# Cosine attention and feed-forward on one core: 64x128 TensorE products cut into 64x64 ones, and an uneven cut of the last output half

## The chip, the core and the metric

The kernel runs on one core of a Trainium2 chip. Its time is the device time of one execution in microseconds; the kernel before takes 405.37 us (median of 3 runs, 405.29 to 405.46). A profile of one execution gives each engine's instructions with their starts: PE is TensorE (PEld its weight loads), DVE is VectorE, ACT is ScalarE, POOL is GpSimd, SP is SyncE, which here only issues transfers.

## What is computed

Eight batches of twelve heads, 448 positions, 64 dimensions a head. Queries and keys are normalised, multiplied, divided by tau = 0.1 and put through a softmax; the result times the values is a matrix of 3584 tokens by 768, which goes through two dense layers with a leaky ReLU between them.

```python
def _attn_ref(q, k, v, tau):
    q_n = q / (np.linalg.norm(q, axis=-1, keepdims=True) + 1e-06)
    k_n = k / (np.linalg.norm(k, axis=-1, keepdims=True) + 1e-06)
    scores = np.matmul(q_n, k_n.transpose(0, 1, 3, 2)) / tau
    scores = scores - np.max(scores, axis=-1, keepdims=True)
    attn = np.exp(scores)
    attn = attn / (np.sum(attn, axis=-1, keepdims=True) + 1e-09)
    return np.matmul(attn, v).astype(np.float32)      # q, k, v: (8, 12, 448, 64)

def _moe_ref(x, w_in, w_out):                         # x: (3584, 768)
    h = x @ w_in                                      # (768, 2048)
    g = np.maximum(0.01 * h, h)
    return (g @ w_out).astype(np.float32)             # (2048, 768)
```

## The kernel before

The order of all work is written out by hand; no planner moves anything. Matrix operands are bfloat16, sums are float32 in PSUM, which is dealt out bank by bank (512 columns of 128 rows, eight banks) by `banks` (L75), the oldest free ones first.

**Heads come in pairs.** A slot s is a pair of heads of one batch; its normalised queries and keys lie transposed in `qkT[s]`, head 0 in rows 0 to 63, head 1 in rows 64 to 127, with 448 query columns (384 and 64) followed by the keys. A *key tile* (`key_tiles`, L268) multiplies a block of keys by all queries of the pair and hands the two banks that it fills to one exponential on ACT (L292). For ki = 0, 1, 2 the block is 128 keys: two matmuls, one per head, with 64 contraction rows and 128 output columns of the array ("64x128"), which run side by side, since they use different rows of the array. For ki = 3 the remaining 64 keys of two neighbouring slots share a tile: four matmuls of 64 rows and 64 columns ("64x64").

**Attention of a batch** (`attend_all`, L675) forms the sums over the exponentials and the products with the values, in matmuls of 64 rows by 32 columns, eight at a time (L719), and then 128 by 32, four at a time (L321). ACT turns the sums into reciprocals, DVE scales into `xT` (L366).

**The dense layers** run by chunks c = 0 to 7 of 384 (even c) or 512 tokens (odd c). The first layer (`first`, L379) accumulates six 128x128 matmuls for each of 16 blocks m of d_ff (L389); ACT applies the leaky ReLU into `hT[c]` (L396). The second layer of chunks 0 to 6 is done in *visits* (`visit`, L776), between the first layer and the next batch's attention. A visit begins with two or three key tiles of kind 3, then interleaves `groups` (L447) with the next batch's 18 key tiles of kinds 0 to 2, at steps listed in `wide`, `three`, `four` and `four_late` (L796 to L799); in the first two visits another key tile of kind 3 stands at the end.

A group takes 128 tokens and both halves of 384 output columns. Each block m of 128 contraction rows is cut in two row halves h, which run side by side into two banks (L464): in the first 16 steps, rows 0 to 63 add to bank 0 and rows 64 to 127 to bank 1; then they change banks, behind a wait on the last matmul of each (L463, `behind`, L205: an empty PE instruction that waits). Two key tiles stand before that wait in every group of this kind. In the first visit two pairs of banks are worked at once, in four parts. At the end DVE or ACT copies the banks out (L476) and SP stores them.

**The last chunk** (c = 7) has no next batch: `second` (L415) runs 128x128 matmuls over 16 blocks (L426), a half of 384 columns at a time, each followed by a DVE copy (L432) and, from the second half on, a store (L441). The very last half is cut into two parts of 192 columns, each copied and stored by itself; of the two transfers of a part, the first is issued on SP and the second on ACT.

**Queues near the change.** PE runs its instructions in the order written, each matmul behind a load of its weights. SP issues the loads of q and k, the transposes by DMA, and the stores. POOL issues the loads of values and weights; the last part of w_out lands while the first visit runs.

Of the kernel before, what the change touches and what calls it, by code (L numbers as in the profile page):

```python
# [16 lines left out]
def kernel(  # L17
# [11 lines left out]
    B, H, S, D = q.shape  # L29
# [12 lines left out]
    HALF = D_model // 2  # L42
# [32 lines left out]
    def banks(count, keep=None, which=None):  # L75
        lo, hi = (0, 8) if not deals["apart"] else (0, 4) if count == 2 else (4, 8)
        x = which if which is not None else min(
            (i for i in range(lo, hi, count) if not set(range(i, i + count)) & set(sum(kept.values(), []))),
            key=lambda i: max(age[i : i + count]),
        )  # L80
        deals["n"] += 1
        age[x : x + count] = [deals["n"]] * count
        if keep:
            kept[keep] = list(range(x, x + count))
        return ps[:, x] if count == 1 else ps[:, x : x + count]

    def given_back(keep):
        deals["n"] += 1
        for i in kept.pop(keep):
            age[i] = deals["n"]  # L90
# [114 lines left out]
    def behind(eng, ins, why):  # L205

        tc.add_manual_dep(
            eng.nop().ins, ins.ins.name,
            mybir.DependencyInfo(mybir.DependencyClass.Sync, mybir.DependencyReason.DATA),
            reason=why,  # L210
        )
# [53 lines left out]
    def scores(s, kis):  # L265
        key_tiles([(s, ki) for ki in kis])

    def key_tiles(which):  # L268

        tiles = []  # L270
        for s, ki in which:
            sc = banks(2)
            tiles.append(sc)
            for i in range(2 if ki == 3 else 1):
                x = qkT[s - 1 + (i ^ s // 2 % NQ % 2)] if ki == 3 else qkT[s]
                for a in range(2):
                    rows = slice(64 * a, 64 * a + 64)
                    out = sc[64 * i : 64 * i + 64] if ki == 3 else sc
                    c0, c1 = (448, 512) if ki == 3 else (512 + 128 * ki, 640 + 128 * ki)
                    nc.tensor.matmul(  # L280
                        out=out[:, a, :S], lhsT=x[rows, c0:c1], rhs=x[rows, 0:S],
                        start=True, stop=True,
                    )
        for (s, ki), sc in zip(which, tiles):
            if ki == 3:
                pr[s // 2] = prp.tile([128, 2, S], BF16, name="pr")
                dst = pr[s // 2]
            else:
                if s not in pe:
                    pe[s] = pep.tile([128, 3, 2, S], BF16, name="pe")  # L290
                dst = pe[s][:, ki]
            nc.scalar.activation(out=dst, in_=sc[:, :, :S], func=AF.Exp, scale=inv_tau)  # L292
# [80 lines left out]
    hT = {}  # L373

    def chunk_cols(c):
        return (0, MAIN) if c % 2 == 0 else (MAIN, 512)
# [27 lines left out]
    def rows_of(c, x, end):  # L404

        bb, rest = divmod(x, S)
        r0 = (2 * (c // 2) + bb) * S
        if rest >= MAIN:
            cnt = min(S - rest, end - x)
            return out[r0 + rest : r0 + rest + cnt], cnt  # L410
        t, p0 = divmod(rest, 128)
        cnt = min(128 - p0, end - x)
        return out[r0 : r0 + MAIN].rearrange("(p t) n -> t p n", t=3)[t, p0 : p0 + cnt], cnt

    def second(c, ts, half):  # L415
        last = c == B - 1 and ts == chunk_cols(c)[1] // 128 - 1
        if half == 0:
            osb[c, ts] = osp.tile([128, D_model], F32, name="osb")
        o = osb[c, ts]
        parts = 2 if last and half == 1 else 1  # L420
        for i in range(parts):
            n = HALF // parts
            lo = half * HALF + i * n
            po2 = banks(1)
            for m in range(MT):
                nc.tensor.matmul(  # L426
                    out=po2[:, :n],
                    lhsT=hT[c][:, m, ts * 128 : (ts + 1) * 128],
                    rhs=w_out_sb[:, m, lo : lo + n],
                    start=(m == 0), stop=(m == MT - 1),  # L430
                )
            nc.vector.tensor_copy(out=o[:, lo : lo + n], in_=po2[:, :n])  # L432
            if half == 1 or last:
                store(o, c, chunk_cols(c)[0] + ts * 128, lo if last else 0, lo + n, parts > 1)

    def store(o, c, x, lo, hi, apart=False):
        end, row = x + 128, 0
        while x < end:
            dst, cnt = rows_of(c, x, end)
            eng = nc.scalar if apart and row else nc.sync  # L440
            eng.dma_start(out=dst[:, lo:hi], in_=o[row : row + cnt, lo:hi])  # L441
            x += cnt
            row += cnt
# [3 lines left out]
    def groups(c, pairs, parts, last):  # L447

        pos2 = [banks(2, ("rows", c, two)) for two in pairs]
        done = [{} for _ in pairs]
        per = MT // parts
        for x in range(2 * parts):
            part, n = divmod(x, 2)
            for p, two in enumerate(pairs):
                if x:
                    for i in range(2):
                        behind(nc.tensor, done[p][i], "the other rows' products in this bank")
                for m in range(part * per, (part + 1) * per):  # L460
                    for h in range(2):
                        rows, i = slice(64 * h, 64 * h + 64), h ^ n
                        ts, half = two[i]  # L463
                        done[p][i] = nc.tensor.matmul(  # L464
                            out=pos2[p][:, i, :HALF],
                            lhsT=hT[c][rows, m, ts * 128 : (ts + 1) * 128],
                            rhs=w_out_sb[rows, m, half * HALF : (half + 1) * HALF],
                            start=(n == 0 and m == 0), stop=(n == 1 and m == MT - 1),
                        )
                    yield  # L470
        for po2, two in zip(pos2, pairs):
            for i, (ts, half) in enumerate(two):
                if (c, ts) not in osb:
                    osb[c, ts] = osp.tile([128, D_model], F32, name="osb")
                copy = nc.scalar.copy if last and i == 0 else nc.vector.tensor_copy
                copy(out=osb[c, ts][:, half * HALF : (half + 1) * HALF], in_=po2[:, i, :HALF])  # L476
                halves_done[c, ts] = halves_done.get((c, ts), 0) + 1
                if halves_done[c, ts] == 2:
                    store(osb[c, ts], c, chunk_cols(c)[0] + ts * 128, 0, D_model)
            given_back(("rows", c, two))  # L480
# [295 lines left out]
    def visit(b, order, norms, between):  # L776


        s0 = (b + 1) * NPAIR
        tiles = [(s0 + p, ki) for p in range(NPAIR) for ki in range(3)]  # L780
        key_tiles([(s0 + 1, 3), (s0 + 3, 3)] + [(s0 + 5, 3)] * (b > 1))
        for i, (pairs, after) in enumerate(zip(order, between)):
            last = i == len(order) - 1
            for n, _ in enumerate(groups(b, pairs, 4 if len(pairs) > 1 else 1, last), 1):
                for _ in range(after.get(n, 0)):
                    key_tiles([tiles.pop(0)])
                for fn in norms.get((i, n), ()):
                    fn()
        assert not tiles
        if b < 2:  # L790
            key_tiles([(s0 + 5, 3)])
# [34 lines left out]
    for b in range(B):  # L826
        tokens = chunk_cols(b)[1] // 128
        if b == B - 1:
            for ts in range(tokens):
                for half in range(2):  # L830
                    second(b, ts, half)
            break
# [78 lines left out]
```

## Time and profile before

| what | value |
|---|---|
| median of 3 runs | 405.37 us |
| profiled execution, its own time | 405.48 us |
| span of its instructions | 403.7 us |
| PE busy | 396.3 us, 98% of the span |
| ACT busy | 264.3 us, 65% |
| DVE busy | 194.5 us, 48% |
| TensorE clock granted | 0.999 |
| L464, second products of the visits | 1536 matmuls, 31% of the chain |
| L280, key tiles | 384 matmuls, 8% of the chain |
| L426, second products of the last chunk | 144 matmuls, 5% of the chain |

The span runs from the first to the last instruction; the 1.8 us by which the time is longer lie around it. A row of the groups gives line, engine, operation, tiles written and read, the array's rows and columns in use ("64*128"), the moving operand's size, the count, then busy time, mean duration of one in ns, and idle time ahead with what ended it. Matmuls overlap one another, so a duration is not the time that a matmul costs; the distance between starts is. "The chain" is the work that ended last, followed back from the end.

### The profile page before, as it was taken

The page shows a single profiled execution, that of the slowest core. Times are in us where ns is not written, and L with a number is a line of the kernel's source. Part 1 is how long each engine was busy: PE and PEld are TensorE (multiplying, and loading weights), DVE is VectorE, ACT ScalarE, POOL GpSimd, SP SyncE. Part 2 cuts the span into 40 slices and gives each one's busy share as a digit, 9 for nine tenths or more (in the row PEclk, how much of TensorE's full clock was granted, in tenths as well). Part 3 has the DMA queues.
Part 4 walks back from the last instruction along what each step waited for, and adds up shares of the span by engine and source line. Part 5 has one row for each costly group of instructions (what it writes and reads, how often), then busy time and mean ns, then how long its engine had stood idle before and what let it go on. Part 6 is the DMA issues. An engine that isn't in the chain of part 4 may idle for free.

```text
span 403.7 us, 10501 instructions
## 1 busy us (share of the span) xinstructions
PE 396.3 (98%) x4254; PEld 224.7 (56%) x4264; DVE 194.5 (48%) x410; ACT 264.3 (65%) x458; POOL 139.5 (35%) x213
## 2 busy tenths in 40 slices
PE   8899999999999999999999999999999999999996
PEld 3335655444555655544886555544687555544564
DVE  6987732783665724464552826276361831140021
ACT  4997799556874689654876469745785559844200
POOL 4995542563344513253140613155122500000000
PEclk9999999999999999999999999999999999999999
DMA  7999999696788827496395944686377721110033
GB/s 191 244 224 239 220 183 227 181 220 145 164 174 148 163 63 176 105 144 176 78 189 119 132 124 119 161 117 147 80 185 112 97 45 41 41 43 0 0 80 78
DMA packets 100736, 54.23 MB, mean 134 GB/s; under 512 B 69424, under 2 KB 95440, under 8 KB 100688
## 3 DMA queue, kind: packets, MB, share of 16 engines
q1 hardware_dynamic: 76400, 40.13, 41.9%
q0 software_dynamic: 23440, 12.92, 23.5%
q8 instruction: 33, 0.54, 0.5%
q10 hardware_dynamic: 848, 0.52, 0.4%
q14 instruction: 15, 0.12, 0.1%
HBM read 45.61 MB, written 11.01 MB: 140 GB/s over the span
## 4 chain that ended last, share of the span: by engine, by line
PE 96%; ACT 2%; DVE 1%; issue 0%
PE ps L389 36%; PE ps L464 31%; PE ps L321 9%; PE ps L280 8%; PE ps L426 5%; PE ps L719 3%; PE ps L510 2%; ACT pe L292 1%; PE ps L236 1%; DVE qkT L261 0%; ACT qkT L553 0%; ACT pr L292 0%; ACT rb L341 0%; DVE warm L493 0%; ACT rb L340 0%
## 5 line engine op out<-in xcount | busy, mean ns | idle before, releaser
L389 PE MATMUL ps<-xT,w_in_sb 128*128 128x384 bf16 (+1 forms) x760 | 147.4, 352 | 0.4
L464 PE MATMUL ps<-w_out_sb,hT 64*128 64x384 bf16 x1536 | 143.9, 323 | 0.0
L292 ACT ACTIVATE pe<-ps 128x896 bf16<-128x896 f32 x144 | 124.4, 917 | 16.7 <-PE ps L280 14.8
L396 ACT ACTIVATE hT<-ps 128x384 bf16<-128x384 f32 (+1 forms) x128 | 67.3, 543 | 73.3 <-PE ps L389 72.8
L389 PEld LDWEIGHTS <-w_in_sb 128*128 128x128 bf16 x768 | 74.1, 98 | 71.5 <-DVE xT L366 2.6
L464 PEld LDWEIGHTS <-hT 64*128 64x128 bf16 x1536 | 84.1, 94 | 45.0 <-PE ps L464 4.2
L182 POOL TENSOR_TENSOR sq<-raw_sb 128x512 f32<-128x512 f32 x90 | 82.0, 932 | 13.6 <-DMA raw_sb<-in_k_dram 13.0
L222 DVE TENSOR_TENSOR qn<-raw_sb,r 128x512 bf16<-128x512 f32 x96 | 55.7, 621 | 1.7
L280 PE MATMUL ps<-qkT 64*128 64x448 bf16 (+1 forms) x384 | 54.7, 353 | 1.6 <-DVE qkT L261 0.8
L193 DVE TENSOR_REDUCE ss<-sq 128x6 f32<-128x384 f32 (+1 forms) x95 | 54.4, 610 | 2.5 <-POOL sq L182 2.3
L476 DVE COPY osb<-ps 128x384 f32<-128x384 f32 x41 | 21.2, 553 | 69.7 <-PE ps L464 38.8
L519 POOL CAST seen<-qn 128x1 f32<-128x1 bf16 x44 | 8.2, 186 | 117.3 <-DVE qn L222 115.3
L217 DVE TENSOR_SCALAR ss<-ss 128x14 f32<-128x14 f32 x48 | 11.5, 239 | 70.6 <-ACT ss L201 70.3
L366 DVE TENSOR_TENSOR xT<-ps,rb 128x448 bf16<-128x448 f32 (+1 forms) x55 | 33.3, 622 | 20.5 <-ACT rb L341 17.8
L160 POOL DMA_DIRECT2D v_b<-in_v_dram x24 | 18.6, 776 | 44.6 <-PE ps L321 44.6
L321 PE MATMUL ps<-pe,v_b 128*32 128x448 bf16 x576 | 30.8, 353 | 0.0
L280 PEld LDWEIGHTS <-qkT 64*128 64x128 bf16 (+1 forms) x384 | 17.7, 97 | 17.9 <-issue 7.0
L321 PEld LDWEIGHTS <-v_b 128*32 128x32 bf16 x576 | 14.5, 97 | 13.4 <-issue 3.2
L432 DVE COPY osb<-ps 128x384 f32<-128x384 f32 (+1 forms) x9 | 4.6, 513 | 36.0 <-issue 22.1
L426 PE MATMUL ps<-w_out_sb,hT 128*128 128x384 bf16 (+1 forms) x144 | 21.0, 308 | 0.0
L292 ACT ACTIVATE pr<-ps 128x896 bf16<-128x896 f32 x24 | 20.7, 924 | 0.2 <-PE ps L280 0.2
L167 POOL DMA_DIRECT2D v_rem<-in_v_dram x32 | 19.8, 641 | 1.6 <-DMA w_out_sb<-in_moe_w_out_dram 1.6
(53 smaller groups left out, 185.7 us busy)
## 6 DMA issues: line engine op xcount, KB each, us to landing
raw_sb<-in_q_dram SPq DMA_DIRECT2D x46, 192.0 KB, 3.1
raw_sb<-in_k_dram SPq DMA_DIRECT2D x44, 192.0 KB, 2.9
out_dram<-osb SPq DMA_DIRECT2D x30, 192.0 KB, 2.8
v_b<-in_v_dram POOLq DMA_DIRECT2D x24, 192.0 KB, 5.1
out_dram<-osb SPq DMA_DIRECT2D x12, 384.0 KB, 3.2
w_out_sb<-in_moe_w_out_dram POOLq DMA_DIRECT2D x4, 768.0 KB, 16.3
w_in_sb<-in_moe_w_in_dram POOLq DMA_DIRECT2D x3, 512.0 KB, 9.5
w_in_sb<-in_moe_w_in_dram POOLq DMA_DIRECT2D x2, 768.0 KB, 13.6
```

What stands on the lines that cost most here:

```text
L182: eng.tensor_tensor(sq, x, x, op=ALU.mult)
L193: nc.vector.tensor_reduce(o.rearrange("p (h t) -> p h t", h=2), sqs[s][i], axis=AX.X, op=ALU.add)
L222: scalings[s] = nc.vector.tensor_tensor(qn[s][:, lo:hi], x.rearrange("p h t d -> p t h d"), r[:, r0 : r0 + 2 * nt].rearrange("p (h t) -> p ...
L280: nc.tensor.matmul(out=out[:, a, :S], lhsT=x[rows, c0:c1], rhs=x[rows, 0:S], start=True, stop=True,)
L292: nc.scalar.activation(out=dst, in_=sc[:, :, :S], func=AF.Exp, scale=inv_tau)
L321: nc.tensor.matmul(out=x[32 * c : 32 * c + 32, :S], lhsT=weights(g, ki) if ki < 3 else rem(g), rhs=pe[s][:, ki, a, :] if ki < 3 else pr[j] ...
L366: scalings[j, e] = nc.vector.tensor_tensor(xT[m][lo:hi, 2 * jj + e, half * S : (half + 1) * S], po[p0 : p0 + hi - lo, :S], rbs[j][lo:hi], ...
L389: nc.tensor.matmul(out=pm[:, :n], lhsT=w_in_sb[:, kt, m * 128 : (m + 1) * 128], rhs=xT[c // 2][:, kt, c0 : c0 + n], start=(kt == 0), stop= ...
L396: nc.scalar.activation(out=hT[c][:, m, :n], in_=pms.pop((c, m))[:, :n], func=AF.Prelu, alpha=0.01)
L426: nc.tensor.matmul(out=po2[:, :n], lhsT=hT[c][:, m, ts * 128 : (ts + 1) * 128], rhs=w_out_sb[:, m, lo : lo + n], start=(m == 0), stop=(m = ...
L464: done[p][i] = nc.tensor.matmul(out=pos2[p][:, i, :HALF], lhsT=hT[c][rows, m, ts * 128 : (ts + 1) * 128], rhs=w_out_sb[rows, m, half * HAL ...
L476: copy(out=osb[c, ts][:, half * HALF : (half + 1) * HALF], in_=po2[:, i, :HALF])
```

## The change

Three things. A key tile of kind 0 to 2 is made of four 64x64 matmuls in place of two of 64x128: its 128 keys are cut into two column halves i, each for both heads. The products of a visit's groups are cut the same way by tokens (t0 = 0 and 64), so that a step is four matmuls in place of two, each into half the rows of its bank; the order within a step is row half h outside, token half t0 inside, while in a key tile it is column half outside, head inside. The last 384 columns of the output are cut into 256 and 128 in place of 192 and 192.

```diff
@@ -267,19 +267,19 @@
     def key_tiles(which):
         tiles = []
         for s, ki in which:
             sc = banks(2)
             tiles.append(sc)
-            for i in range(2 if ki == 3 else 1):
+            for i in range(2):
                 x = qkT[s - 1 + (i ^ s // 2 % NQ % 2)] if ki == 3 else qkT[s]
+                c0 = 448 if ki == 3 else 512 + 128 * ki + 64 * i
                 for a in range(2):
                     rows = slice(64 * a, 64 * a + 64)
-                    out = sc[64 * i : 64 * i + 64] if ki == 3 else sc
-                    c0, c1 = (448, 512) if ki == 3 else (512 + 128 * ki, 640 + 128 * ki)
                     nc.tensor.matmul(
-                        out=out[:, a, :S], lhsT=x[rows, c0:c1], rhs=x[rows, 0:S],
-                        start=True, stop=True,
+                        out=sc[64 * i : 64 * i + 64, a, :S], lhsT=x[rows, c0 : c0 + 64],
+                        rhs=x[rows, 0:S], start=True, stop=True,
                     )
         for (s, ki), sc in zip(which, tiles):
             if ki == 3:
@@ -417,10 +417,9 @@
         if half == 0:
             osb[c, ts] = osp.tile([128, D_model], F32, name="osb")
         o = osb[c, ts]
-        parts = 2 if last and half == 1 else 1
-        for i in range(parts):
-            n = HALF // parts
-            lo = half * HALF + i * n
+        widths = (HALF * 2 // 3, HALF // 3) if last and half == 1 else (HALF,)
+        for i, n in enumerate(widths):
+            lo = half * HALF + sum(widths[:i])
             po2 = banks(1)
             for m in range(MT):
                 nc.tensor.matmul(
@@ -431,7 +430,7 @@
                 )
             nc.vector.tensor_copy(out=o[:, lo : lo + n], in_=po2[:, :n])
             if half == 1 or last:
-                store(o, c, chunk_cols(c)[0] + ts * 128, lo if last else 0, lo + n, parts > 1)
+                store(o, c, chunk_cols(c)[0] + ts * 128, lo if last else 0, lo + n, len(widths) > 1)
     def store(o, c, x, lo, hi, apart=False):
         end, row = x + 128, 0
@@ -445,6 +444,7 @@
     halves_done = {}
     def groups(c, pairs, parts, last):
@@ -458,12 +458,12 @@
                     for i in range(2):
                         behind(nc.tensor, done[p][i], "the other rows' products in this bank")
                 for m in range(part * per, (part + 1) * per):
-                    for h in range(2):
+                    for h, t0 in ((0, 0), (0, 64), (1, 0), (1, 64)):
                         rows, i = slice(64 * h, 64 * h + 64), h ^ n
                         ts, half = two[i]
                         done[p][i] = nc.tensor.matmul(
-                            out=pos2[p][:, i, :HALF],
-                            lhsT=hT[c][rows, m, ts * 128 : (ts + 1) * 128],
+                            out=pos2[p][t0 : t0 + 64, i, :HALF],
+                            lhsT=hT[c][rows, m, ts * 128 + t0 : ts * 128 + t0 + 64],
                             rhs=w_out_sb[rows, m, half * HALF : (half + 1) * HALF],
                             start=(n == 0 and m == 0), stop=(n == 1 and m == MT - 1),
                         )
```

## The prediction

> **What bounds the kernel now.** I read the page first: engine shares, the chain that ended last, the DMA queues.
>
> ```profile
> PE 396.3 (98%) x4254; PEld 224.7 (56%) x4264; DVE 194.5 (48%) x410; ACT 264.3 (65%) x458; POOL 139.5 (35%) x213
> ...
> q8 instruction: 33, 0.54, 0.5%
> ...
> PE 96%; ACT 2%; DVE 1%; issue 0%
> PE ps L389 36%; PE ps L464 31%; PE ps L321 9%; PE ps L280 8%; PE ps L426 5%; PE ps L719 3%; PE ps L510 2%; ACT pe L292 1%; PE ps L236 1%; DVE qkT L261 0%; ACT qkT L553 0%; ACT pr L292 0%; ACT rb L341 0%; DVE warm L493 0%; ACT rb L340 0%
> ```
>
> TensorE is the bound, and both changed products (L464, L280) are on the chain. So what counts is the spacing of matmul starts. Then the groups by shape:
>
> ```profile
> L464 PE MATMUL ps<-w_out_sb,hT 64*128 64x384 bf16 x1536 | 143.9, 323 | 0.0
> L280 PE MATMUL ps<-qkT 64*128 64x448 bf16 x288 | 47.9, 350 | 1.6 <-DVE qkT L261 0.8 <-ACT pe L292 0.5 <-ACT qkT L553 0.2
> L280 PE MATMUL ps<-qkT 64*64 64x448 bf16 x96 | 6.9, 361 | 0.0
> ```
>
> "323" is a latency. Read by single starts, a pair on the two row halves starts every 162.5 ns at 384 columns and every 189.3 ns at 448. I call that a pass. L464 is 768 passes x 162.5 = 124.8 us, against 31% of 403.7 = 125.
>
> Third, the timeline where a visit begins (the third, then the fourth):
>
> ```profile
> 144.28 0.76 PE L280 MATMUL ps<-qkT 64*64 64x448 bf16 x12
> 144.39 0.49 ACT L396 ACTIVATE hT<-ps 128x384 bf16<-128x384 f32 x1 [0.48 <-PE ps L389]
> ...
> 144.98 0.50 PE L464 MATMUL ps<-w_out_sb,hT 64*128 64x384 bf16 x4
> ```
> ```profile
> 191.31 0.60 ACT L396 ACTIVATE hT<-ps 128x512 bf16<-128x512 f32 x1 [0.70 <-PE ps L389]
> ...
> 191.90 0.54 PE L464 MATMUL ps<-w_out_sb,hT 64*128 64x384 bf16 x4
> ```
>
> Already here four 64x64 products run at a time: passes at 144.285, 144.498, 144.688, the last step 190 ns. Then the first 64x128 pass comes 291 ns later, 102 more than a pass: the array drains when the shape changes. Every change of shape shows it: 93 ns when the old shape's streams are level, plus any lag of its last stream. The second block shows 0.54 in place of 0.50: rows 64 to 127 wait for the bank that ACT frees at 191.91, start at 191.963, and stay 47 ns late to the visit's end, where the change of shape takes 137 instead of 92.
>
> **The change, part by part** (against the profiled run: span 403.7, its time 405.48, 0.11 above the median 405.37).
>
> *Number of passes.* L464 becomes 3072 matmuls in 768 fours; key tiles 576 in 144 fours. Columns per stream are the same, so the passes cost nothing more if fours keep pace: 190 ns above against 189.3. At the other end, 1 ns per pass would be 0.9 us.
>
> *Visit starts.* The change 64x64 to 64x128 goes, seven times 102 ns. What is late next is ACT. In visits 1 and 2 other banks are used and the last stream gains 95 (102 less 7, four starts being 3.3 ns apart): 0.19 us. In visits 3, 5 and 7 ACT ends at 144.88, its bank is seen free some 52 ns later (191.911 to 191.963), so the late rows gain only 144.983 - 144.94 = 43 each: 0.13. In 4 and 6 they already wait for ACT: nothing. Gain 0.32.
>
> *Visit ends.* In visits 1 and 2 a 64x64 key tile stands behind 64x128 work; its 93 goes, and 22 of its single pass's exposed load: 2 x 115 = 0.23. The change into L719's 64x32 stays. Gain at both ends: 0.55 us.
>
> *Order of starts.* New. A key tile runs row half by row half within a column half; a four of L464 runs column half by column half within a row half. The 47 ns above were kept for a hundred passes, each start in program order. If a start may not overtake the one before it and needs 3.3 ns behind it (the spacing inside each four), every swap of order makes the fourth stream 3.3 ns later, for good, since each stream begins when its own last one is done. The visits have 17, 14, 15, 14, 15, 14 and 15 places where key tiles are put in, two swaps each, plus 9 at their ends: 217 x 3.3 = 0.72 us, collected at the seven drains. The low end is nothing, if streams of other columns may pass. I take 0.72, as every start in the trace keeps the order.
>
> The Trainium skill, "TensorE: Matmul & The Clock Gate", section on packing small matmuls, says that matmuls start and end strictly in program order. By it the sum has the 0.72; without it the sum would be lower by that much. The 47 ns lag agrees, but no swap is in this trace.
>
> *Half-way waits.* A group waits once for its other rows (L463); two key tiles cover it, and matmul starts show no loss. But the two loads behind it come 32 ns apart (148.092, 148.124), with the matmul due at 148.158. Four come at .092, .124, .156, .188, and the fourth matmul some 16 ns later, at .204 against a due .168: 36 ns once per visit (afterwards the stream is late anyway, and the wait fits behind it). Five visits: 0.18; with the swaps' lag already there, 0.10. Bounds: 0, and 22 groups x 36 = 0.8. A 64x64 load is 105 ns against 94, hidden under a pass; behind these waits uncovered it would add 22 x 13 = 0.3.
>
> *Head.* 18 key tiles before 31 us. A pass alone costs 316 with its drain in 64x64, 296 to 299 in 64x128: +18; behind another, +11. Thirteen such places are 0.19; those before 25 us stand ahead of waits for ACT or DVE. The four after it give 0.065. I take 0.11.
>
> *Tail.*
>
> ```profile
> 399.23 1.75 ACTq L441 DMA_DIRECT2D out_dram<-osb  x2
> 400.09 0.36 DVE L432 COPY osb<-ps 128x192 f32<-128x192 f32 x1 [0.89 <-PE ps L426]
> ```
>
> 16 x 109.3 + 16 x 55.9 (256 columns by the law of the passes; 128 from the transposes' starts at L236) against 32 x 82.6: both 2.64. The last copy falls from 358 to about 292 (556 at 384 columns, 358 at 192: 1.03 ns a column), gain 0.07. The earlier copy now ends at about 399.69, its two stores hold SP until about 400.40, and the last copy ends at 400.38: just clear. Bounds: -0.15 with smaller packets, +0.1 if the queue is late.
>
> *Sum.* -0.55 + 0.72 + 0.10 + 0.11 - 0.07 = +0.31: the profiled run would be 405.8, the median 405.7.
>
> **The rivals.**
>
> *B, no price for swaps.* -0.55 + 0.18 + 0.11 - 0.07 = -0.33: 405.0. For it: streams are independent once started. Against: no overtaking anywhere in the trace.
>
> *C, instructions come too late.* This is slower, by one mechanism in the first visit. 0.54 MB in 33 packets is 16 KB each; about 8500 PE instructions make one per 256. Now a block lasts 64 passes, 10.4 us; with fours 32, 5.2 us.
>
> ```profile
> 50.50:69.50 19.00, 19.00 (x232) 11.02 (x228) 5.25 (x12) 17.56 (x23) 5.20 (x9) 1.00 1.33 200
> 97.60:121.70 24.10, 24.10 (x294) 14.09 (x292) 13.31 (x30) 19.00 (x29) 8.68 (x13) 1.00 0.74 160
> ```
>
> The last column but one is the DMA share: visit 1 runs under full queues. Counted by executed loads and matmuls, the packet at 385.4 starts 117 past a multiple of 256, the one at 60.5 starts 288 past: some 160 instructions x 40.6 = 6.5 us later, and it takes 1.46. If only one block is held ahead, 8.0 against 5.2 is a stall of up to 2.8 us for each of two or three blocks, less the matmuls queued: +2 to +6, 407.4 to 411.4. It decides from the point where a block takes over 5.2 us to come; visits 2 to 4, at a share of 0.5 to 0.75, come out at 2 to 4 by the same count. Against: the depth of the store is unseen, and with more blocks held nothing happens.
>
> The Trainium skill, "Runtime: NRT & Kernel Launch", section on instruction fetch, gives blocks of 256 instructions and speaks of two lines, but also of 2048 instructions for PE. By two, C holds; by eight, not. The 33 packets agree with the block; the depth no run here shows.
>
> *D, the sequencer can't hand out eight instructions per pass.*
>
> ```profile
> 162.21 1.95 PE ps L464 x24
> 164.16 2.02 PE ps L719 x80
> ```
>
> L719's 160 instructions in 2.02 us are 12.6 ns each, but a queue may have been full; L321 behind it needs 23.6 for longer. The restart gives 16 (32 for two). Fours need 20.3. At 21 a pass is 168: 768 x 5.5 = +4.2 us; at 20.8, +3: 406 to 410. It decides from 20.3.
>
> **How the numbers follow.** Slipping order 0.36 (0.33 within 0.2%, 0.03 slower); B 0.24 (0.17 within, 0.07 faster); C 0.24 and D 0.11, slower; something unlisted 0.05 (0.03 faster, 0.02 slower). 0.2% is 0.8 us, about what a measurement can tell from no change. Faster 0.10, within 0.50, slower 0.40. The likeliest case gives 405.7, its own range 405.2 to 406.3 from the bounds of waits, head and tail. The whole range must take in C's lower half and most of B and D: 404.7 to 409.2, leaving out about 0.04 of B below and 0.14 of C and D above.
>
> **What would show it.** No 102 ns drain ahead of L464, and in visits 4 and 6 the rows 64 to 127 still at ACT's release. Fourth-stream lag rising by 6.7 ns at each key tile, to about 0.1 us at a visit's end: the order slips; level, B. PE idle in 50 to 70 us beside q8 packets: C. L464 starts further apart than 162.5 in all visits: D. Wrong outright: fours that don't run together over long stretches, or a drain inside a visit.

## The result and the profile after

The changed kernel takes 410.28 us (median of 6 runs, 408.38 to 411.4) against 405.33 (6 runs, 405.27 to 405.46): 1.0114 times as long, 95% interval 1.0089 to 1.0139. Times are medians; ratios, here and below, are estimated from all the runs and need not be the quotient of two medians. The profiled execution took 410.19, its span is 408.4. The runs of the changed kernel spread over 3 us, those of the kernel before over 0.2.

From the page of the changed kernel: engines, the instruction queue, the chain, the second products.

```profile
PE 398.7 (98%) x6088; PEld 264.5 (65%) x6088; DVE 194.6 (48%) x410; ACT 263.7 (65%) x458; POOL 139.5 (34%) x213
...
q8 instruction: 47, 0.77, 0.8%
...
PE 93%; ACT 2%; issue 1%; DMA 1%; POOL 1%; DVE 1%; POOLq 0%
...
L464 PE MATMUL ps<-w_out_sb,hT 64*64 64x384 bf16 x3072 | 149.0, 325 | 2.6 <-issue 2.6
```

TensorE still carries the chain, but "issue" has grown in it from 0 to 1%, and L464 has 2.6 us of idle time that no semaphore ended. Instruction packets went from 33 to 47. To see where the time came in, I compare the starts of each stage in the two traces (first matmul of a visit, of the attention behind it, and so on):

| stretch | longer by, us |
|---|---|
| start to first visit | -0.28 |
| first visit | +5.28 |
| visit 2 | -0.16 |
| visits 3, 5, 7 | -0.03 each |
| visits 4, 6 | +0.03 each |
| attention and first layer, together | +0.04 |
| last chunk and end | -0.14 |

So everything is lost in one visit. Its chain of waits:

```profile
57.04 0.18 PE ps L280
57.22 0.54 issue
57.77 0.36 PE ps L280 x2
...
63.13 0.18 PE ps L464 x2
63.31 2.60 issue
65.91 2.29 PE ps L464 x29
```

Twice TensorE stands with nothing to wait for. The first stop cuts a key tile in two (one of its four matmuls starts at 56.87, the other three at 57.77), the second cuts a step of L464: no semaphore lies there. Counting the executed TensorE instructions, the first stop comes after 1217 and the second after 1473: exactly 256 apart. By the trace's record of single packets, a 16 KB instruction packet landed at 56.50, 1.27 us before the first restart, and the next at 64.45, 1.46 before the second. Between them the whole cycle can be read: a block begins to run at 57.77, the packet that holds the one after it starts only at 63.50, 5.7 us later (when it was asked for isn't recorded), takes 0.95, and work goes on at 65.91. That is 8.1 us for a block whose instructions started within 5.2 (57.77 to 62.99). Counted the same way, for blocks that begin inside visits 2 to 7, the packet with the next block starts between 1.2 us before and 1.5 us after the first instruction of the current one. So a block is fetched while the one before it runs, and not earlier.

The third part of the loss stands in the windows. A row gives the window and its length, then busy time and count of instructions for PE, PEld, DVE, ACT and POOL; the last three columns are granted clock, DMA share (the time that packets took, as a share of 16 engines' time; packets overlap, so it can pass 1) and GB/s:

```profile
56.00:62.80 6.80, 6.26 (x150) 4.87 (x146) 1.06 (x2) 5.31 (x7) 0.18 (x1) 1.00 1.48 164
62.80:65.90 3.10, 0.51 (x11) 0.11 (x3) 1.02 (x2) 1.23 (x2) 0.00 (x0) 1.00 1.49 123
65.90:69.80 3.90, 3.89 (x56) 3.09 (x59) 1.02 (x2) 0.92 (x1) 0.84 (x1) 0.56 1.14 309
69.80:75.00 5.20, 5.20 (x125) 4.55 (x117) 0.01 (x1) 4.89 (x7) 2.80 (x4) 1.00 0.21 81
```

After 2.9 us of idleness the granted clock is 0.56 over the next 3.9 us, and from 66.3 to 69.8 passes start 320 ns apart in place of 162.5. By the spacing of starts the two stops cost 3.7 (some 0.8 and 2.9) and the slow clock 1.7; less some 0.15 that the visit gains elsewhere, that is the 5.28. Five of the six runs have a mean granted clock of 0.994 to 0.996 (this one 0.995); the sixth, at 0.999, is the shortest, 408.38.

### The profile page after: what moved, and what is told of

Same layout as the page of the kernel before. It is cut to its first block, busy times and chain, and to the rows that moved or that the text cites. A ratio compares the mean times of both kernels' runs of the same rounds, so it can differ in the third digit from the quotient of the medians.

```text
span 408.4 us, 14177 instructions
## 1 busy us (share of the span) xinstructions
PE 398.7 (98%) x6088; PEld 264.5 (65%) x6088; DVE 194.6 (48%) x410; ACT 263.7 (65%) x458; POOL 139.5 (34%) x213
## 4 chain that ended last, share of the span: by engine, by line
PE 93%; ACT 2%; issue 1%; DMA 1%; POOL 1%; DVE 1%; POOLq 0%
PE ps L389 36%; PE ps L464 31%; PE ps L321 9%; PE ps L280 8%; PE ps L425 5%; PE ps L719 3%; ACT pe L292 1%; DMA raw_sb<-in_k_dram 1%; PE ps L236 1%; POOL raw_sb L132 0%; DVE qkT L261 0%; DVE qn L222 0%; POOL sq L182 0%; ACT pr L292 0%; POOL v_b L160 0%
## 5 line engine op out<-in xcount | busy, mean ns | idle before, releaser
L464 PE MATMUL ps<-w_out_sb,hT 64*64 64x384 bf16 x3072 | 149.0, 325 | 2.6 <-issue 2.6
L464 PEld LDWEIGHTS <-hT 64*64 64x64 bf16 x3072 | 119.9, 107 | 15.2 <-PE ps L464 3.7
L280 PE MATMUL ps<-qkT 64*64 64x448 bf16 x672 | 62.1, 355 | 1.7 <-DVE qkT L261 0.6
L280 PEld LDWEIGHTS <-qkT 64*64 64x64 bf16 x672 | 26.5, 107 | 12.5 <-issue 7.6
L431 DVE COPY osb<-ps 128x384 f32<-128x384 f32 (+2 forms) x9 | 4.6, 513 | 35.9 <-issue 22.1
L425 PE MATMUL ps<-w_out_sb,hT 128*128 128x384 bf16 (+2 forms) x144 | 21.0, 308 | 0.0
```

Source lines behind the costliest of these rows:

```text
L280: nc.tensor.matmul(out=sc[64 * i : 64 * i + 64, a, :S], lhsT=x[rows, c0 : c0 + 64], rhs=x[rows, 0:S], start=True, stop=True,)
L425: nc.tensor.matmul(out=po2[:, :n], lhsT=hT[c][:, m, ts * 128 : (ts + 1) * 128], rhs=w_out_sb[:, m, lo : lo + n], start=(m == 0), stop=(m = ...
L464: done[p][i] = nc.tensor.matmul(out=pos2[p][t0 : t0 + 64, i, :HALF], lhsT=hT[c][rows, m, ts * 128 + t0 : ts * 128 + t0 + 64], rhs=w_out_sb ...
```

## The experiments

Theory S: TensorE holds one block of 256 instructions ahead of the one in work; where the DMA queues are full, the next comes later than fours use one up. Rivals stand with the runs. e1 to e4 ran on one chip, where the kernel before took 405.46 (404.98 to 406.23), and e5 to e8 on another, where it took 405.45 (405.21 to 406.19); each ratio is against its own chip. The diffs show the main lines; "..." stands for lines left out. The stage differences below compare profiles with that of the kernel before.

**e1. First visit in pairs, the rest as changed.** Against the changed kernel:

```diff
+    PAIRS = (0,)
...
-            for i in range(2):
+            whole = pairs and ki < 3
+            for i in range(1 if whole else 2):
...
-                    for h, t0 in ((0, 0), (0, 64), (1, 0), (1, 64)):
+                    for h, t0 in ((0, 0), (1, 0)) if c in PAIRS else ((0, 0), (0, 64), (1, 0), (1, 64)):
...
-                    key_tiles([tiles.pop(0)])
+                    key_tiles([tiles.pop(0)], b in PAIRS)
```

> The changed kernel, but the first visit's key tiles and second products run as 64x128 pairs again. Theory S (TensorE runs out of instructions in the first visit: one block of 256 is held ahead, and with full DMA queues the next one comes too late): no TensorE idle time in the first visit, and the time is that of the kernel before less what the other parts gain: 0.28 in the head, 0.16 in the second visit, 0.04 in visits 3 to 7, 0.14 in the tail, so 404.7 to 405.0 us. Rival P (fours as such are slower, by dispatch or in the array): six of seven visits still hold fours, so most of a loss that is spread over the visits stays, and the time is over 408.

Measured: 405.31 us, ratio 1.0001 (0.9993 to 1.0010). The first visit is as long as before to 0.001 us, visits 2 to 7 show the same differences as in the table, the span is 403.4. The whole loss is gone with the fours of one visit, and fours in six others cost nothing: P falls. Yet the small gains don't show in the times, and the median misses the 404.7 to 405.0 that S gave: 8 of 12 runs lie at 405.1 to 405.4, four at 405.7 to 406.5.

**e2. Fours in the first visit alone.** Against the kernel of e1:

```diff
-    PAIRS = (0,)
+    PAIRS = (1, 2, 3, 4, 5, 6)
...
-        key_tiles([(s, ki) for ki in kis])
+        key_tiles([(s, ki) for ki in kis], True)
...
-        widths = (HALF * 2 // 3, HALF // 3) if last and half == 1 else (HALF,)
+        widths = (HALF // 2, HALF // 2) if last and half == 1 else (HALF,)
```

> The kernel before with fours in the first visit alone (key tiles and second products); head, visits 2 to 7 and tail as before. Theory S: the whole loss is here, +4 to +6 us, 409 to 411, spread widely from run to run, with TensorE idle at two places 256 TensorE instructions apart. Rival P: about a seventh of the loss, 405.5 to 406.5.

Measured: 408.51 us, ratio 1.0076 (1.0059 to 1.0093), a little under what S gave; the first visit is 3.32 us longer and all other visits are within 0.001. Two of its stops are of the known kind (after 1473 and 1729 instructions, again 256 apart). The longest is not:

```profile
61.23 0.52 PE L468 MATMUL ps<-w_out_sb,hT 64*64 64x384 bf16 x8 [1.32 <-DMA w_out_sb<-in_moe_w_out_dram]
```

Here a quarter of w_out landed late. None of the three stops is as long as the 2.9 us above, and the mean clock is 0.999. That the place is right is shown; that starvation is all there is to this place is not, since full queues delay data too.

**e3. Emptier queues, the same TensorE instructions.** Against the changed kernel:

```diff
-    load_w_out(range(0, MT, MT // 4))
+    load_w_out(range(0, MT // 4, MT // 4))
...
+    for m in range(MT // 4, MT, MT // 4):
+        nc.vector.tensor_copy(out=w_out_sb[:, m : m + MT // 4], in_=w_out_sb[:, : MT // 4])
```

> The changed kernel with three of the four loads of w_out left out: the second to fourth quarter of w_out in SBUF are copies of the first, made by VectorE, so the output is not the reference's. All TensorE instructions and their order stay. Theory S: queues are light by 50 us, instruction packets come within 2 us of their request, and the first visit has no stall: 404.5 to 405.2 us. Rival P, and a rival W by which the stall comes from the fours' own waits in the first visit (banks, the half-way waits): the stall stays at 3 us or more, over 408 us.

Measured: 406.46 us, ratio 1.0023 (1.0007 to 1.0038), runs from 404.81 to 407.97. The windows of its first visit show why it lies between the two numbers:

```profile
48.00:52.00 4.00, 4.00 (x58) 2.47 (x60) 3.14 (x7) 3.37 (x8) 4.00 (x6) 1.00 0.22 24
52.00:56.00 4.00, 4.00 (x104) 2.80 (x100) 3.19 (x6) 3.80 (x7) 3.66 (x4) 1.00 1.24 130
56.00:60.00 4.00, 2.98 (x73) 2.01 (x69) 1.31 (x3) 2.30 (x3) 0.18 (x1) 1.00 1.65 118
60.00:64.00 4.00, 4.00 (x98) 3.21 (x91) 0.15 (x1) 3.67 (x4) 0.00 (x0) 1.00 0.76 197
```

The queues were not empty between 52 and 60 us: loads of q, k and v fill them (share 1.24 and 1.65), and there TensorE stops once, after 1217 instructions, for 1.2 us more than a pass. From 60 us the share is 0.76, and where the next block ends, after 1473, 0.2 us is lost. My expectation that the queues would be light was wrong; that the stop follows them, block by block, supports S. The first visit is 1.33 us longer than before in this profile.

**e4. The last output half alone.** Against the kernel before:

```diff
-        parts = 2 if last and half == 1 else 1
+        widths = (HALF * 2 // 3, HALF // 3) if last and half == 1 else (HALF,)
```

> The kernel before with the last 384 columns cut into 256 and 128 alone. By the copy (1.03 ns a column) the gain is 0.07 us; by the profile of the changed kernel, whose stretch from the last chunk to the end is 0.135 us shorter, 0.13. Both: 405.2 to 405.3 us. If the earlier part's stores held SP, no gain.

Measured: 405.31 us, ratio 0.9995 (0.9986 to 1.0003). The times can't tell it from nothing; in the profiles the last stretch is 0.16 us shorter. Over all profiles, the stretch from the last chunk to the end differs by 0 to -0.02 where the cut is 192 and 192, and by -0.14 to -0.16 in six of the seven with 256 and 128 (+0.01 in the seventh).

**e5. One order of starts.** Against the kernel of e1:

```diff
-            for i in range(1 if whole else 2):
-                for a in range(2):
+            for a, i in ((0, 0), (1, 0)) if whole else ((0, 0), (0, 1), (1, 0), (1, 1)):
```

> The changed kernel with its first visit in 64x128 pairs (as in e1), and key tiles issued row half outside, column half inside, the order that the second products have. Theory O (a start may not overtake the one before it in the program, so every swap of order costs 3.3 ns for good): visits 2 to 7 end with their last stream about 0.1 us less late, some 0.6 us in all against e1. Theory I (the four streams run by themselves): visits 2 to 7 as in e1 within 0.02 us each, 405.2 to 405.4 us.

Measured: 405.56 us, ratio 1.0006 (0.9997 to 1.0015). Visits 2 to 7 differ from those of the pairs by -0.159, -0.032, +0.032, -0.032, +0.031 and -0.032; with swaps they were -0.156, -0.033, +0.031, -0.032, +0.032 and -0.032. Swaps cost nothing, and theory O falls. One stop of 0.2 us stands in the attention behind the fifth visit (restart at 259.60, packet landed at 258.21).

**e6. One half-way wait in place of two.** Against the kernel of e1:

```diff
-                    for i in range(2):
-                        behind(nc.tensor, done[p][i], "the other rows' products in this bank")
+                    behind(nc.tensor, done[p][n], "the other rows' products in both banks")
```

> The kernel of e1, with one wait in place of two at the half-way point of a group: on the last matmul of the half alone. Theory H (behind the first of the two waits the sequencer hands over nothing, so the four loads come 32 ns apart and the fourth stream is some 60 ns late from there to the end of the visit): the change of shape behind visits 3 to 7 falls from 156 to 158 ns to about 105, 0.05 us a visit, 0.3 us in all: 404.9 to 405.1 us. Rival: the lag comes from the bank that ACT frees at the start of a visit or from the order of starts, and stays: no difference from e1.

Measured: 405.86 us, ratio 1.0010 (0.9999 to 1.0022). The loads behind the wait do come 3 ns apart now (third visit: 147.736, .739, .742, .746), but visits 3 to 7 are as long as in e1 to 0.002 us. H was wrong on the loads as well: in e1 only the first two stand 33 ns apart (147.864, .897, .901, .904), not all four, and only the first two streams start late for it, by 16 and 13 ns. The fourth stream ends a visit; it is some 85 ns late from the visit's second pass on in both kernels, and the waits don't change that. The median lies 0.55 us above that of e1, for which these visits give no cause; single runs went from 405.17 to 407.52, and the profiled one took 405.31.

**e7 and e8. The cause carried to another visit.** Two kernels, that of e1 (fours from the second visit on) and the kernel before (pairs), with the same added load:

```diff
+    scratch = cpool.tile([128, 2, MT // 4, 736], BF16, name="scratch")
...
+        if b == 2:
+            hold(hT[b][:, MT - 1, 0:1])
+            for i in range(2):
+                gp.dma_start(out=scratch[:, i], in_=w_out_r[:, 0 : MT // 4, 0:736])
         visit(
```

> The kernel of e1 with two loads added that nobody reads: at the start of the third visit GpSimd's queue fetches 736 columns of a quarter of w_out into a scratch tile, twice. Theory S (fours starve where the queues are full): TensorE stops in the third visit, 1 to 6 us in all, at places 256 TensorE instructions apart, and the time is 406.5 to 411 us. Rival F (something else of the first visit makes the stall: cold start, two pairs of banks at a time, w_out landing late): no stop, 405 to 406 us.

> The kernel before (pairs everywhere) with the same two loads at the start of the third visit. Both theories: TensorE does not stop in the third visit, 405.3 to 406 us; a stop here would mean that the added loads delay data that the kernel needs.

Measured: with fours 407.0 us, ratio 1.0048 (1.0031 to 1.0064); with pairs 405.48, ratio 1.0002 (0.9993 to 1.0011). The windows of the third visit, fours first:

```profile
157.00:161.00 4.00, 3.34 (x84) 2.45 (x79) 1.59 (x4) 2.92 (x5) 2.36 (x3) 1.00 1.07 209
161.00:165.00 4.00, 3.79 (x91) 2.45 (x84) 0.00 (x0) 3.32 (x4) 0.00 (x0) 1.00 1.27 291
```
```profile
157.00:161.00 4.00, 4.00 (x54) 2.34 (x49) 1.81 (x4) 3.79 (x5) 2.59 (x4) 1.00 1.14 245
161.00:165.00 4.00, 4.00 (x72) 2.21 (x76) 0.56 (x1) 3.16 (x5) 0.00 (x0) 1.00 1.35 179
```

At nearly the same DMA share, TensorE is busy without a break in pairs and stops in fours. The stops:

```profile
159.26 0.36 PE L470 MATMUL ps<-w_out_sb,hT 64*64 64x384 bf16 x4 [0.66 <-issue]
...
165.25 0.48 PE L470 MATMUL ps<-w_out_sb,hT 64*64 64x384 bf16 x5 [0.46 <-issue]
```

They come after 4284 and 4540 instructions, 256 apart once more; the packets landed at 157.75 and 163.98, 1.5 and 1.3 us ahead of the restarts. The visit is 1.63 us longer than the same visit in e1. This is the strongest of the runs: nothing of the first visit is needed, only full queues and eight instructions per pass. Rival F falls.

## Why the prediction was wrong, point by point

- **The sum.** It gave 405.7, and the likeliest case was 0.2% around no change; measured was 1.1% slower, above the top of the range. The step that failed: the sum put the wait for instructions at nothing (its passes "cost nothing more if fours keep pace"), and rival C, which is that wait, got a chance of only 0.24. In the first visit the fours didn't keep pace: two stops of 3.7 us in all, and 1.7 of slow clock behind them. C's mechanism was right: the blocks, 5.2 us to use one up, the place, and a price of 2 to 6 us. That its 8.0 us to get a block comes so near the 8.1 measured is in part luck: C added 6.5 us of lateness and 1.46 of transfer; measured were 5.7, 0.95, and 1.46 from landing to restart, which C did not have. I left C at 0.24 because the trace of before could not show how many blocks are held. The stops 256 apart, each ended by the packet just landed, and packets that start only about when the block before them begins, show one. The Trainium skill, "Runtime: NRT & Kernel Launch", section on instruction fetch, has both readings, two lines and 2048 instructions; these runs agree with the first. That section of the Trainium skill also remarks that fetching is hidden by the rate of issue; with full queues this does not hold here, at eight instructions in 162.5 ns.
- **A term that C lacked.** I let a stop cost its own length. The long one was followed by a slow clock, which cost another 1.7 us, and with it the time passed the range. Behind stops of 0.7 to 1.6 us there was none (granted clock 1.00 in the windows of e2, e3 and e7).
- **Order of starts, +0.72.** Wrong, it is nothing (e5). The four streams need not hold program order. From the timeline of the changed kernel, behind the first stop, which left the streams up to 185 ns apart:

```profile
62.12 0.81 PE L464 MATMUL ps<-w_out_sb,hT 64*64 64x384 bf16 x13
...
62.62 0.35 PE L280 MATMUL ps<-qkT 64*64 64x448 bf16 x1
...
62.64 0.33 PE L464 MATMUL ps<-w_out_sb,hT 64*64 64x384 bf16 x2
...
62.77 0.38 PE L280 MATMUL ps<-qkT 64*64 64x448 bf16 x3
```

  The key tile's first matmul starts at 62.62, ahead of two of L464 that stand before it in the program. I had read "kept in order" from streams that were never more than 47 ns apart, a fraction of a pass, where nothing could overtake. The Trainium skill, "TensorE: Matmul & The Clock Gate", section on packing small matmuls, says that matmuls start in program order; here they don't, and the measurement decides.
- **Visit starts and ends, -0.55.** Of this, 0.34 fell to visits 2 to 7, measured 0.19. The drain ahead of L464 is gone as predicted, and ACT's release of the bank is what comes next, as predicted. Mis-sized is the fourth stream: it starts its second pass 27 ns after the third (lags 0, 7, 56 and 83 ns in the third visit of e1), as its first matmul, whose load nothing covers, is that much longer (347 ns against 320); the sum let it go along with the third. So visits 3, 5 and 7 gain 0.03 and not 0.04, and visits 4 and 6 lose 0.03.
- **Half-way waits, +0.10.** Nothing (e6). The sum took the four loads to come 32 ns apart each; in the changed kernel only the first two do (third visit: 152.913, .946, .949, .953), and the streams that they hold up are not the one that ends the visit.
- **Head, +0.11.** Not seen. The stretch to the first visit is between -0.28 and +0.13 in six profiles with fours there and between -0.16 and +0.30 in four with pairs: it varies by more than the term.
- **Tail, -0.07.** Right in sign, -0.14 to -0.16 in size. The copy fell from 0.36 to 0.29 us as worked out; the rest lies behind it, where from the copy's end to the end of the span it took 3.19 us after 3.25. I had that only as a bound. The line of the last copy after the change:

```profile
404.94 0.29 DVE L431 COPY osb<-ps 128x128 f32<-128x128 f32 x1 [0.40 <-PE ps L425]
```

- **Rival B** is right that swaps cost nothing; e1 comes nearest to its case (405.31, where B gave 405.0). **Rival D** is excluded: passes keep 162.5 ns through visits 2 to 7, at eight instructions each.
- **What would show it** had named C's sign, idle time between 50 and 70 us beside instruction packets, and it came out.

## What to carry to other kernels

Cutting matmuls into smaller ones that run side by side kept the array's time here (a pass of 162.5 ns) and doubled the instructions. Work out how long one 16 KB block of 256 then lasts, and compare it with the time from the start of a block until the next can run (in the changed kernel 6 and 8 us in the first visit, where the DMA queues are full, and 1 to 4 in visits 2 to 7). Look for that in the kernel as it is, by counting executed instructions at each instruction packet: lateness is visible before it costs anything (in the kernel before, the packet at 60.51 starts some 4.2 us into a block that lasts 10.5). Here the small gains (0.2 us at changes of shape, 0.14 in the tail) were not worth the risk: even with the first visit in pairs, no version was measurably faster than the kernel before.

## What the runs showed that I had not expected

TensorE idle for 2.9 us was followed by 3.5 us at half pace (320 ns a pass); no run tests that link by itself. An instruction packet needs another 1.3 to 1.6 us from landing to the first matmul of its block, in each of the stops at the end of a block (changed kernel, e2, e3, e5, e7). Fours also leave the attention behind a visit short of instructions at times: stops of 0.1 to 0.3 us stand there in the profiles of e3, e5 and e7. Whether such stops make the slower third of e1's runs, or the slow runs of e5 and e6, was not tried.
